# Loads, decay rounds and TensorE's order moved in a kernel of RWKV-7 attention and hash routing

## The chip, the cores and the metric

The kernel runs on one core of a Trainium2 chip. The metric is the device time of one execution in microseconds, the median of three runs. A core has five engines that run side by side, each with its own queue of instructions in order: TensorE (PE in the profile; its weight loads are PEld), VectorE (DVE), ScalarE (ACT), GpSimd (POOL) and SyncE (SP). Transfers are issued from the queues of SyncE, GpSimd and ScalarE and run on sixteen DMA engines.

## The reference, cut to what matters

Two blocks follow each other. The first is a recurrence over 768 tokens for 4 x 8 heads with 40 x 40 states:

```python
def _attn_ref(r, k, v, w, a, b):
    state = np.zeros((B, H, D, D), dtype=np.float32)        # B, H, S, D = 4, 8, 768, 40
    for t in range(S):
        kt, vt, rt = (k[:, :, t], v[:, :, t], r[:, :, t])
        wt, at, bt = (w[:, :, t], a[:, :, t], b[:, :, t])
        y[:, :, t] = np.einsum('bhd,bhde->bhe', rt, state)
        Sa = np.einsum('bhde,bhe->bhd', state, at)
        state_decay = state * wt[:, :, None, :] - np.einsum('bhd,bhe->bhde', Sa, bt)
        state = state_decay + np.einsum('bhd,bhe->bhde', vt, kt)
    return y
```

The second sends each of the 3072 rows to one of 8 experts by a hash of its token and applies two layers, `np.maximum(xe @ w1[e], 0.0) @ w2[e]`, with w1 320 x 1024 and w2 1024 x 320. The change touches the first block alone.

## The kernel before

The recurrence is computed in chunks of 64 tokens. A *tile* is one chunk of two batches (128 partitions); there are 24 of them. A tile passes two halves. The first half forms `at` and `z` (a, b and k multiplied by products of decays), turns both on TensorE, forms the scores `a` between tokens, and with three other tiles (a *group*) inverts the triangular part of the scores on VectorE. The second half follows 8 *ticks* later: it applies the inverse, updates the state and makes the output y. So for 24 ticks TensorE does the second half of one tile beside the first half of the tile that is 8 later.

All steps are entered in a plan with a tick, and the plan is then sorted, so that a number decides where a step stands in each engine's queue. `STEPS` gives the places within a tick:

```python
STEPS = ["r1", "z", "y", "nc", "x", "at_t", "x_t", "s", "u", "sd", "a", "r_t", "r0", "rc"]

def at_tick(tick, step=None, order=0):
    if step is not None:
        tick += STEPS.index(step) / len(STEPS)
    ...
# [cut]
with tc.manual_schedule(engines={ET.PE, ET.DVE, ET.Activation, ET.Pool}):
    for *_, f in sorted(plan, key=lambda e: e[:3]):
        f()
```

The products of decays, p and q, are made for two chunks at a time, in 6 *rounds*. A round loads w, multiplies up a tree (`todo`), gets the other half's product by a small matmul (`f_ps`), and goes down the tree again for p and for q (`then`). Round 0 keeps p and q in SBUF for tiles 0 to 3 and stores p for later; the other rounds store both to DRAM, from where the tiles load them:

```python
def decays(ri, t_w, t0, span, t_f, span_f=None, stores=None):
    ...                                         # [cut] load w; todo: the products, up to x["own"]
    @then.append
    def _():
        x["f_ps"] = p = bank([P, D], "f_ps")
        nc.tensor.matmul(p, lhsT=partner[:], rhs=x["own"][:], start=True, stop=True)
    ...                                         # [cut] ends, reciprocal, spread of pb
    @then.append
    def _():
        spread(x["pb"], True, (0,))
        if ri == 0:
            x["p"] = p_rows = turned_rows(x["pb"][:], early.tile([P, 2 * BLK * BLK], F32, tag="nu", name="p_rows"))
            at_tick_later.append(lambda: nc.sync.dma_start(pq_dram[ri][0].rearrange("t bh e -> t (bh e)"), p_rows))
        elif stores is None:
            store(0, x["pb"][:])
    ...                                         # [cut] the same for q; en_ps and pend
    if ri == 0:
        then = then[:3] + then[5:7] + then[3:5] + then[7:]
        at_tick_later = []
        at_tick(1.36)(lambda: [f() for f in at_tick_later])
    if stores is not None:
        at_tick(stores)(lambda: (store(0, x["pb"][:]), store(1, x["qb"][:])))
    for i, f in enumerate(todo):
        at_tick(t0 + span * i / len(todo), order=8)(f)
    for i, f in enumerate(then):
        at_tick(t_f[i] if isinstance(t_f, tuple) else t_f + span_f * i / len(then), order=8)(f)
```

The inputs of a tile are six transfers on SyncE's queue, 64 x 8 pieces of 40 numbers each. Two tiles borrow buffers that later steps use:

```python
    @at_tick({0: -3.9, 1: -3.8, 2: -2.8, 3: -2.7}.get(u, max(u - 2.55, t_mult_of(u - 2) + 0.03)))
    def _():
        kb_tag = {2: "x_t", 3: "mr"}.get(u)
        ...                                     # [cut] kb from tag kb_tag or "kb" (2 buffers)
        x["a"] = al = work.tile([P, DM], F32, tag="py" if kb_tag else "al", name="al")
        load(lambda be, rows: by_head(al, rows), a, 2 * g, n * C)
        load(lambda be, rows: by_head(kb[:, be], rows), b, 2 * g, n * C)
        load(lambda be, rows: by_head(kb[:, be], rows), k, 2 * g, n * C, crossed=True)
```

The inversion of a group takes the single buffer `nu`, which is also the buffer of `row` and of round 0's `p_rows`:

```python
def group_i(gi, t0, t1, t2):
    @at_tick(t0 - 0.5, order=9)
    def _():
        x["nu"] = nu = early.tile([P, 2, BLK * BLK], F32, tag="nu", name="nu")
        ...                                     # [cut]
        nc.gpsimd.memset(ub, 0.0)
    @at_tick(t0, order=9)
    def _():
        nc.vector.transpose(paired(x["n"])..., paired(x["pk"])...)
    ...                                         # [cut] 30 pairs: outer = u * n; u += outer; then ut
# [cut]
for gi in range(NU // GRP):
    t0 = gi * GRP + GRP - 1 + t_a               # t_a = STEPS.index("a") / len(STEPS)
    group_i(gi, t0 + 0.05, t0 + 0.1, t0 + 3.4)
```

In a tick with both halves TensorE's chain is: rc (scores of r with x), which VectorE masks to `mr`; y, which needs `mr` and `sd`; nc, which needs the copy `r1`; x and u (the inverse); x_t (x turned, after ScalarE has copied it out of nc); s (the state, which VectorE multiplies to `st`); sd (`st` turned); a (which needs `z_t` and `at_t`), of which ScalarE copies `pk` and `no` and VectorE masks `mk`. Of the PSUM buffers, z, nc, x_t, sd, a and rc share two of two banks each, in turn.

## Time and profile before

| | us |
|---|---|
| median of 3 runs | 647.45 |
| lowest, highest | 645.55, 648.0 |
| span of the profiled run | 645.1 |

| engine | busy us | share |
|---|---|---|
| TensorE, matmul | 556.3 | 86% |
| TensorE, weight loads | 422.7 | 66% |
| VectorE | 351.6 | 55% |
| ScalarE | 293.7 | 46% |
| GpSimd | 195.8 | 30% |

The page divides the span into 40 slices of 16 us and gives the busy share of each in tenths; TensorE has 4 to 6 in slices 2 to 5 and 8 or 9 from slice 7 on. In the first slices the granted clock of TensorE falls to 0.5. "Releaser" in the views below is what ended an engine's wait; "issue" is time in which the engine waited for nothing that the profile shows. A row of a timeline has the start, the length, the engine, the line, what it does, and in brackets the idle time before it.

### The profile page before, as it was taken

How to read it: one execution, taken by the hardware profiler on the slowest of the kernel's cores; microseconds unless marked ns; L12 is line 12 of the kernel's file. 1: busy time of each engine (PE TensorE's matmuls, PEld its weight loads, DVE VectorE, ACT ScalarE, POOL GpSimd, SP SyncE). 2: the span in 40 equal slices, each digit the busy share in tenths (PEclk: the TensorE clock that was granted, in tenths of full speed). 3: DMA queues.
4: the chain of work that ended last, by engine and by line, in shares of the span. 5: the costliest groups of instructions: out<-in, count | busy, mean ns of one | idle time of the engine just before them, and what ended most of it. 6: DMA issues, size and time to landing. Idle time of an engine off the chain costs nothing.

```text
span 645.1 us, 22962 instructions
## 1 busy us (share of the span) xinstructions
PE 556.3 (86%) x9866; PEld 422.7 (66%) x9866; DVE 351.6 (55%) x920; ACT 293.7 (46%) x695; POOL 195.8 (30%) x331
## 2 busy tenths in 40 slices
PE   0443568988999999999899998999999999999995
PEld 0332457877787878888788887666565646565552
DVE  6968679966977896797798553232021202203010
ACT  4162436757776677777767661113131304101100
POOL 0631341535333344432423321261313131230101
PEclk9975559989999999999999999999999999999999
DMA  8999988987797687842434613697333373220000
GB/s 160 198 197 178 163 154 143 190 144 137 149 184 148 129 169 149 153 97 45 103 60 116 155 53 97 223 290 248 110 102 113 105 264 103 66 96 20 30 12 25
DMA packets 195770, 85.13 MB, mean 132 GB/s; under 512 B 176718, under 2 KB 186191, under 8 KB 195664
## 3 DMA queue, kind: packets, MB, share of 16 engines
q1 hardware_dynamic: 184016, 45.59, 37.6%
q0 software_dynamic: 11456, 37.37, 20.1%
q8 instruction: 78, 1.28, 0.9%
q10 hardware_dynamic: 192, 0.66, 0.4%
q14 instruction: 28, 0.23, 0.1%
HBM read 66.54 MB, written 15.40 MB: 127 GB/s over the span
## 4 chain that ended last, share of the span: by engine, by line
PE 50%; issue 23%; DVE 10%; DMA 6%; SPq 5%; POOL 4%; ACT 2%; POOLq 0%; DVEq 0%; ACTq 0%
PE up_ps L1057 6%; PE dn_ps L1075 6%; PE y_ps L291 5%; PE s_ps L291 4%; PE rc_ps L291 3%; PE r_ps L291 3%; SPq L310 3%; PE x_t_ps L733 3%; PE a_ps L291 3%; PE t_ps L573 3%; PE sd_ps L793 3%; PE z_ps L521 2%; POOL out_dram L1080 2%; DVE mr L745 2%; PE nc_ps L291 2%
## 5 line engine op out<-in xcount | busy, mean ns | idle before, releaser
L1065 DVE TENSOR_SCALAR ht<-up_ps 128x416 f32<-128x416 f32 (+2 forms) x36 | 19.4, 543 | 165.2 <-PE up_ps L1062 163.7
L1075 PE MATMUL dn_ps<-w,ht 128*128 128x320 f32 x336 | 91.7, 433 | 0.0
L1057 PE MATMUL up_ps<-xt,w 128*128 128x416 f32 x224 | 81.3, 516 | 0.0
L1075 PEld LDWEIGHTS dn_ps<-w,ht 128*128 128x128 f32 x336 | 63.3, 190 | 25.5
L1080 POOL DMA_INDIRECT out_dram<-o,idx_all x26 | 26.1, 1004 | 165.4 <-ACT o L1079 164.3
L785 POOL DMA_DIRECT2D x_rows<-xs x44 | 23.2, 535 | 171.3 <-DVE xs L781 96.5
L1067 ACT ACTIVATE ht<-up_ps 128x416 f32<-128x416 f32 (+2 forms) x36 | 17.2, 478 | 107.5 <-PE up_ps L1062 107.4
L1057 PEld LDWEIGHTS up_ps<-xt,w 128*128 128x128 f32 x224 | 41.9, 190 | 36.8 <-issue 31.7
L615 DVE TENSOR_TENSOR outer<-nu 128x252 f32<-128x252 f32 (+8 forms) x180 | 63.4, 352 | 4.9
L622 DVE TENSOR_TENSOR nu<-nu,outer 128x252 f32<-128x252 f32 (+8 forms) x180 | 63.4, 352 | 4.3
L1079 ACT COPY o<-dn_ps 128x320 f32<-128x320 f32 x26 | 11.1, 425 | 92.4 <-PE dn_ps L1075 92.4
L521 PE MATMUL z_ps<-ident,z 128*104 128x128 f32 x192 | 31.2, 315 | 24.2 <-DVE z L507 21.4
L525 ACT COPY z_t<-z_ps 104x512 f32<-104x512 f32 x48 | 25.7, 588 | 47.4 <-PE z_ps L521 46.3
L521 PEld LDWEIGHTS z_ps<-ident,z 128*104 128x104 f32 x192 | 24.5, 150 | 27.1 <-issue 23.2
L468 POOL DMA_DIRECT2D ql<-q_rows x48 | 25.1, 531 | 48.4 <-DVE pb L377 15.4
L723 ACT COPY x<-nc_ps 64x320 f32<-64x320 f32 x48 | 20.1, 420 | 42.7 <-PE nc_ps L291 42.1
L745 DVE TENSOR_TENSOR mr<-rc_ps,after 128x1024 f32<-128x1024 f32 x24 | 29.3, 1220 | 13.6 <-PE rc_ps L291 13.6
L291 PE MATMUL rc_ps<-r_t,x_t 64*64 64x64 f32 x1536 | 30.1, 222 | 6.7 <-issue 6.0
L291 PE MATMUL a_ps<-at_t,z_t 64*64 64x64 f32 x1536 | 32.3, 241 | 3.6 <-ACT at_t L574 2.4
L291 PEld LDWEIGHTS a_ps<-at_t,z_t 64*64 64x64 f32 x1536 | 28.6, 152 | 8.1 <-ACT at_t L574 3.6
L548 DVE TENSOR_TENSOR mk<-a_ps,after 128x512 f32<-128x512 f32 x24 | 16.6, 690 | 28.9 <-ACT no L565 26.2
L291 PEld LDWEIGHTS rc_ps<-r_t,x_t 64*64 64x64 f32 x1536 | 25.7, 134 | 9.3 <-issue 6.1
(230 smaller groups left out, 1125.9 us busy)
## 6 DMA issues: line engine op xcount, KB each, us to landing
ql<-q_rows POOLq DMA_DIRECT2D x48, 160.0 KB, 4.3
w<-in_moe_w_dram SPq DMA_DIRECT2D x10, 640.0 KB, 7.6
w<-in_moe_w_dram SPq DMA_DIRECT2D x10, 512.0 KB, 4.3
al<-in_a_dram SPq DMA_DIRECT2D x48, 80.0 KB, 4.2
pl<-p_rows POOLq DMA_DIRECT2D x48, 80.0 KB, 4.5
r<-in_r_dram SPq DMA_DIRECT2D x48, 80.0 KB, 3.8
x<-in_v_dram SPq DMA_DIRECT2D x48, 80.0 KB, 3.7
py<-p_rows POOLq DMA_DIRECT2D x48, 80.0 KB, 4.8
```

The lines of the kernel that those rows point to most:

```text
L291: nc.tensor.matmul(out_, lhsT=lhsT, rhs=rhs, start=start, stop=stop, skip_group_check=True)
L468: nc.gpsimd.dma_start(ql[half(be)], of_batches(rows_of_chunk("q"), 2 * g, 2))
L521: nc.tensor.transpose(p[0:R, be, hp * P:(hp + 1) * P], x["z"][:, be, hp, :], ident[:])
L525: nc.scalar.copy(t[0:R, be].rearrange("p h t -> p (h t)"), p[0:R, be])
L615: nc.vector.tensor_tensor(tv, paired(x["u"])[:, 0:full[1], j:j + 1, :].to_broadcast(full), paired(x["n"])[:, j // 2, j + 1:, j % 2].unsque ...
L622: nc.vector.tensor_tensor(o, o, x["t"][:, 0:n].rearrange("p (c i k) -> p c i k", c=full[1], k=2), op=OP.add)
L723: nc.scalar.copy(x["x"][half(be), be].rearrange("p (a q) (two e) -> p a (q two) e", a=2, two=2)[:, :, :, 0:D], p[half(be), :, 0:HP * D].re ...
L745: nc.vector.tensor_tensor(t[:].rearrange("p two h t -> p (two h) t"), p[:].rearrange("p two (h t) -> p (two h) t", t=C), after[:].unsqueez ...
L785: dma(x_of[2 * g + be, n * C:(n + 1) * C], xs[half(be), :])
L1057: nc.tensor.matmul(p[:], lhsT=w1[c][:, (f0 + i) * P:(f0 + i + 1) * P], rhs=xt[:, c, 0:n], start=(c == 0), stop=False)
L1075: nc.tensor.matmul(p[i * m:(i + 1) * m], lhsT=ht[:, f, c0:c0 + m], rhs=w2[f // (FP // 2)][:, f % (FP // 2), :], start=(f == 0), stop=(f == ...
L1080: st = nc.gpsimd.indirect_dma_start(out=out[:], out_offset=bass.IndirectOffsetOnAxis(ap=idx, axis=0), in_=o[0:m], in_offset=None, bounds_c ...
```

## The change

It moves steps in the plan; the arithmetic is the same. The inputs of tiles 4 to 7 are to be loaded at the time of the first tiles, with the borrowed buffers used a second time by tiles 6 and 7; the store of round 0's p goes behind them. Rounds 3 to 5 of the decays are to stand between two inversions instead of within one. On TensorE, z of the next tile goes between r0 and rc, at_t to the place behind r1, and sd between x and x_t.

```diff
-    STEPS = ["r1", "z", "y", "nc", "x", "at_t", "x_t", "s", "u", "sd", "a", "r_t", "r0", "rc"]
+    STEPS = ["r1", "at_t", "y", "nc", "x", "sd", "x_t", "s", "u", "a", "r_t", "r0", "z", "rc"]
...
-            at_tick(1.36)(lambda: [f() for f in at_tick_later])
+            at_tick(3.2)(lambda: [f() for f in at_tick_later])
...
-            at_tick(t_f[i] if isinstance(t_f, tuple) else t_f + span_f * i / len(then), order=8)(f)
+            at_tick(t_f + span_f * i / len(then) if span_f else t_f[i], order=8)(f)
...
     def t_mult_of(u):
-        return u + LATE[u] - 0.1 if u in LATE else u - 0.6
+        return u + LATE[u] - 0.2 if u in LATE else u - 0.6
...
-        @at_tick({0: -3.9, 1: -3.8, 2: -2.8, 3: -2.7}.get(u, max(u - 2.55, t_mult_of(u - 2) + 0.03)))
+        @at_tick({0: -3.9, 1: -3.8, 2: -2.8, 3: -2.7, 4: 0.9, 5: 1.5, 6: 2.0, 7: 2.5}.get(u, max(u - 2.55, t_mult_of(u - 2) + 0.03)))
         def _():
-            kb_tag = {2: "x_t", 3: "mr"}.get(u)
+            kb_tag = {2: "x_t", 3: "mr", 6: "x_t", 7: "mr"}.get(u)
...
-        @at_tick(u - 0.4 if ahead else u + late, None if ahead else "z")
+        @at_tick(u - 0.4 if ahead else u - 1 + late, None if ahead else "z")
...
     for ri in range(3, NR):
-        t0 = ri * RN * NG - 5.0
-        decays(ri, t0 - 2.0, t0 + 0.25, 1.0, t0 + 1.3, 1.1)
+        t0 = ri * RN * NG - 4.9
+        decays(ri, t0 - 2.1, t0, 0.12, [t0 + f for f in (0.13, 0.2, 0.21, 0.25, 0.35, 0.42, 0.5, 0.55)])
```

## The prediction

> **What bounds the kernel now.** I read the page's first two parts, then the busy time by stretches, then the timelines of single engines, and the table of waits last. The stretches, each row with its length and then the busy microseconds of TensorE, its weight loads, VectorE, ScalarE and GpSimd:

> ```profile
> core 0: us, PE busy (x) PEld busy (x) DVE busy (x) ACT busy (x) POOL busy (x), PEclk, DMA share, GB/s
> 0.00:47.00 47.00, 15.03 (x313) 12.95 (x313) 34.75 (x98) 20.13 (x62) 15.11 (x34) 0.94 0.98 184
> 47.00:88.00 41.00, 16.44 (x246) 14.30 (x248) 32.04 (x80) 14.11 (x34) 9.60 (x20) 0.50 0.97 162
> ...
> 262.00:310.00 48.00, 46.41 (x1366) 40.13 (x1368) 37.72 (x94) 35.89 (x85) 17.32 (x34) 1.00 0.46 88
> ...
> 395.00:645.00 250.00, 239.80 (x1018) 148.43 (x1018) 46.93 (x146) 46.44 (x94) 61.97 (x70) 0.99 0.38 122
> ```

> There are three regimes. Up to about 88 us VectorE leads (78% busy from 47 to 88 us, TensorE 40%). From 110 to 395 us TensorE is nearly full. The last 250 us are the expert layers, whose instructions the change leaves in the same order on TensorE. So the time is about: when TensorE becomes dense, plus its work and its stalls in the ticks, plus 250.

> The start, on the queue of SyncE, on GpSimd and on VectorE (start, length, engine, line, what; in brackets the idle time before and its releaser):

> ```profile
> 34.71 4.63 SPq L339 DMA_DIRECT2D q_rows<-qb  x4
> 39.39 1.71 SPq L408 DMA_DIRECT2D p_rows<-p_rows  x1
> 41.15 1.67 SPq L310 DMA_DIRECT2D al<-in_a_dram  x2
> ```
> ```profile
> 44.63 0.95 POOL L591 MEMSET nu<- 128x1024 f32 x1 [1.22 <-DMA p_rows<-p_rows]
> ```
> ```profile
> 46.98 1.25 DVE L597 STREAM_TRANSPOSE nu<-pk 128x1024 f32<-128x1024 f32 x1 [1.21 <-ACT pk L564]
> ...
> 78.85 0.49 DVE L500 SCALAR_TENSOR_TENSOR at<-al,pl 128x320 f32<-128x320 f32 x1 [3.26 <-DMA al<-in_a_dram]
> 81.31 0.83 DVE L507 TENSOR_TENSOR z<-kb,ql 128x640 f32<-128x640 f32 x1 [1.97 <-DMA kb<-in_k_dram]
> ...
> 87.62 1.20 DVE L631 STREAM_TRANSPOSE ut<-nu 128x1024 f32<-128x1024 f32 x1
> ```

> The first inversion runs on VectorE from 46.98 to 88.82 us. In it VectorE waits 3.26 + 1.97 = 5.2 us for the inputs of tile 7. And the buffer `nu` of the inversion is the buffer that held p of round 0: GpSimd's clearing of it waited for the store of p (line 408) to land, at 44.6 us, 5.2 us after its issue began. That wait was harmless.

> TensorE's waits from 88 to 310 us (in total, times, longest):

> ```profile
> PE r_ps L291 <- issue: 5.7, 4, 2.0
> PE rc_ps L291 <- issue: 5.3, 6, 2.3
> PE x_ps L291 <- DVE ut L630: 3.5, 1, 3.5
> PE y_ps L291 <- DVE mr L745: 1.9, 3, 1.0
> ```

> Only 1.9 us are for mr. The large entries, "issue", break off in the middle of a group (rc stops after 53 of its 64 at 133.8 us), so they aren't data.

> [...]78 instruction packets carry 1.28 MB, and the stalls stand where a, r0, rc and r1 use up instructions fastest. [...]0.50 from 47 to 88 us, and after the 2.26 us stall at 133.8 us eight z transposes took 1.88 us instead of 1.01. [...]

> **The change part by part.** No instruction is added or removed; everything is order.

> 1. Inputs of tiles 4 to 7 at ticks 0.9 to 2.5. Removes VectorE's waits for tile 7: -5.2 us. The z of tiles 4 to 6 stand slightly earlier against the inversion, which I put at -0.4 us of the 1.66 us that mk waits there (1.08 and 0.58), but the mk of tile 6, which used to be hidden behind the wait for tile 7, then waits about 0.5 us. Net -5.1.

> 2. The store of p moves from tick 1.36 to 3.2. In the built program it stands on SyncE's queue behind the loads of tiles 4 to 7 and the stores of round 1, and the inversion's first transpose (line 597) waits for its completion. Step by step: tile 4's loads wait for the at of tile 0, done at 26.4 us; six DMAs at about 0.7 us each, to 31. The stores of round 1's p take 4.2 us as now, to 35.2; its q 4.6 to 5, to 40. Then the loads of tiles 5, 6 and 7, which take 4.0 to 5.9 us a tile in this trace (tiles 0 to 3: 4.0 to 4.8), so 3 x 4.6 = 14, to 54. Then the store, 5.2 us to its landing: 59 (57 to 62). VectorE is ready for line 597 at about 47.6, so it sits idle for some 11 us, and the inversion starts 12 us late. With part 1 it ends at 88.8 + 12 - 5.1 = 95.7 us: +6.9.

> 3. Rounds 3 to 5 of the decays between inversions. VectorE's work in a round, by the rows of round 1 (22.18 to 34.60 us): products 2.5, ends 0.9, p 2.2, q 2.2, so about 7.8 us. It now stands in a block behind ut, where VectorE used to idle (3.61 us before mk at 95.2, 3.30 at 149.5), which is the aim. But the small matmul f_ps, which needs the products, now stands on TensorE right after nc and before x. In a steady tick, counted from the end of rc: TensorE reaches f_ps after r1 0.70, at 0.58, y 1.61 and nc 0.60, at 3.5 us. VectorE has mr to 1.2, two last small steps, ut 2 x 1.2 to 4.2 (at 136.5 to 140.6 it took just that), products 2.5 and xs 0.45: 7.1 us. So TensorE stalls 3.6 us[...]. Then mk and the next transposes come late: VectorE's block ends 14.7 us after rc, so rc, which now takes over the PSUM buffer of a, waits some 0.3 us, and mr 0.3 more. I put 5 us on each of rounds 4 and 5, less 0.9 of "issue" stall[...]: +8. In round 3, at the start, x of tile 0 begins 3.0 us after ut instead of 1.07 before its end; the at transpose of tile 7 (1.1) now lies ahead, and z of tile 8 as before. Along xi, um (1.7), u, a, r_t, r0, z, r1, at and nc at half clock I get nc 14.9 us after ut, against 9.3 plus the 0.6 of at: +5.

> 4. Order on TensorE. A tick's own work doesn't change: r1 0.70, at 0.58, y 1.61, nc 0.60, x 0.62, sd 0.82, x_t 0.87, s 1.28, u 0.62, a 1.09, r_t 0.59, r0 0.70, z 1.01, rc 1.09 = 12.2 us. The 16 ticks from 106.8 to 314.6 us took 13.0 each; some 0.8 is stall. With z between r0 and rc, two stretches of many short matmuls are parted by 1 us with few instructions, and r_t has longer to be copied. I expect a third to a half of the "issue" stalls to go: -5. sd between x and x_t covers the 0.86 us copies of x, which matters in the last eight ticks: -1.5.

> Sum: 6.9 + 5 + 8 - 5 - 1.5 = +13.4, so 647.5 + 13.4 = 661.

> **The rivals.** First, the store lands early enough, because SyncE's queue runs faster than I reckon. For it: SyncE idles from 21 to 30 us. Against: 18 loads lie between the q stores and the store of p, and none in this trace went faster than 0.63 us in a row, so even then it isn't issued before 51 us and lands at 56: 3 us less, 658. Second, the stalls at f_ps don't come, because VectorE runs ahead: before, it waits 24.5 us in all for a's copies ahead of mk. Against: that wait ties it to TensorE in the very tick before ut. Without the stalls: 653. Third, the order on TensorE frees all of the 5.7 + 5.3 + 1.9 = 12.9 us of stalls before r, rc and y; with the second rival that would be 653 - (12.9 - 5) = 645. Fourth, a late first tick that also delays the fetch and holds the clock at half for longer: 670.

> **Range and chances.** The delay of the first inversion is seen in the program's waits and is nearly certain; its size is 10 to 15. The stalls at f_ps are reckoned, 0 to 12. The gain on TensorE is the least sure, 0 to 12. Together 648 to 672. The line of +2% is 660.4, just below my number: slower by over 2% 0.52, within 2% 0.42, faster by over 2% 0.06.

> **What would show it.** Right: line 597 starts near 59 us with a wait on the DMA of p_rows; no VectorE wait for al or kb up to 96 us; f_ps waits for own about 3.5 us three times; mk has hardly any waits in those ticks; the first y at about 120 us rather than 108. Wrong: line 597 near 47 us, or TensorE without waits on own, or ticks without "issue". If the first y comes before 108 us, the whole of the first half is wrong, and the time falls below 640.

## The result, and the profile after

| | before | after |
|---|---|---|
| median, us | 647.73 | 665.62 |
| lowest, highest, us | 645.55, 648.74 | 663.64, 667.06 |
| ratio (95% interval) | | 1.0279 (1.0241 to 1.0317) |

The change costs 18 us, 2.8%. The busy time by stretches of the kernel after, with the same columns as in the prediction (stretch, length, busy microseconds of TensorE, its weight loads, VectorE, ScalarE and GpSimd, granted clock, DMA):

```profile
0.00:61.00 61.00, 16.25 (x312) 14.26 (x312) 34.80 (x97) 21.16 (x64) 13.16 (x30) 0.84 0.95 173
61.00:98.00 37.00, 17.22 (x241) 15.04 (x241) 32.56 (x80) 13.65 (x32) 11.57 (x23) 0.50 0.85 148
272.00:320.00 48.00, 46.91 (x1440) 40.59 (x1436) 40.09 (x97) 36.98 (x87) 17.75 (x35) 1.00 0.54 106
415.00:665.00 250.00, 239.80 (x1018) 148.35 (x1018) 47.03 (x146) 46.48 (x94) 62.03 (x70) 1.00 0.38 122
```

The expert layers took their 250 us as before. In the first 61 us each engine does about what it did in the first 47 us before; those 14 us are idle. SyncE's queue shows why (start, length, engine, line, what):

```profile
29.86 1.36 SPq L310 DMA_DIRECT2D kb<-in_k_dram  x2
31.32 6.97 SPq L339 DMA_DIRECT2D p_rows<-pb  x4
38.39 4.79 SPq L339 DMA_DIRECT2D q_rows<-qb  x4
43.23 1.75 SPq L310 DMA_DIRECT2D al<-in_a_dram  x2
...
55.60 1.31 SPq L310 DMA_DIRECT2D kb_mr<-in_k_dram  x2
56.96 0.62 SPq L408 DMA_DIRECT2D p_rows<-p_rows  x1
```

The store of round 0's p is issued at 56.96 us, behind three tiles of loads. GpSimd's clearing of `nu`, and then VectorE's first transpose of the inversion, wait for it to land:

```profile
61.13 0.95 POOL L591 MEMSET nu<- 128x1024 f32 x1 [13.83 <-DMA p_rows<-p_rows]
```
```profile
61.12 1.25 DVE L597 STREAM_TRANSPOSE nu<-pk 128x1024 f32<-128x1024 f32 x1 [12.73 <-DMA p_rows<-p_rows]
...
97.10 1.20 DVE L631 STREAM_TRANSPOSE ut<-nu 128x1024 f32<-128x1024 f32 x1
```

Before, line 597 stood at 46.98 us with a wait of 1.21; the inversion ends at 98.3 us instead of 88.8. No wait of VectorE for `al` or `kb` is left in it. TensorE's waits from 98 to 320 us (in total, times, longest):

```profile
PE f_ps L384 <- DVE own L365: 11.7, 3, 5.3
PE rc_ps L291 <- issue: 3.6, 3, 2.0
...
PE r_ps L291 <- issue: 0.9, 2, 0.6
...
PE y_ps L291 <- DVE mr L745: 0.6, 2, 0.3
```

The three stalls at `f_ps` are there, and the entries "issue" have shrunk. What an "issue" stall waits for can be read from the same traces. In the kernels before and after, the instruction packets of the queue q8 are of 16 KiB (78 of them, 1.28 MB in all); 40 come between 120 and 310 us, one every 4.8 us. In these two kernels all 24 such stalls of TensorE between 100 and 400 us end 1.2 to 1.7 us after the transfer of such a packet has ended; in the fourteen traces of this case 145 of 164 do, while of the matmuls without a stall only about one in nine starts at such a moment. By this timing they are waits for instructions, as the prediction took them to be.

The loss is best laid out between three marks: the first `mr` of VectorE (the start), the sixteenth (the middle, ticks with both halves; 24 tiles that are 8 apart give 16 of these, not 24), and the first matmul of the experts (the tail, in which the first half of the tiles has run out). Before, the start took 108.9 us, the middle 205.8, the tail 81.2. What the kernels of the main comparison took more or less than that, in microseconds of one profiled execution, with "issue" stalls and half-clock time in the middle:

| kernel | start | middle | tail | issue, middle | half clock, middle |
|---|---|---|---|---|---|
| before | 0 | 0 | 0 | 13.4 | 3.4 |
| after | +13.1 | +2.9 | +4.1 | 5.8 | 6.8 |
| TensorE's order alone | +0.4 | +4.8 | +5.6 | 6.0 | 17.1 |
| decays alone | +2.8 | +2.5 | +4.4 | 5.8 | 13.7 |
| loads and store alone | +8.6 | -2.1 | +4.8 | 10.3 | 0 |
| loads alone | -4.0 | -3.6 | +3.5 | 8.5 | 0 |
| after, store back | -0.8 | +4.6 | +6.6 | 6.2 | 10.2 |

Two kernels that share their code up to a mark still differ there: three kernels with the start of "after" reached the first `mr` at 119.2, 119.7 and 122.0 us, and from there to the fifteenth, again with the same code, they took 193.3, 191.6 and 194.3 us. So a difference under 3 us in one cell says nothing by itself.

### The profile page after: what moved, and what is told of

It is laid out like the page before. It is cut to its first block, busy times and chain, and to the rows that moved or that the text cites. A ratio compares the mean times of both kernels' runs of the same rounds, so it can differ in the third digit from the quotient of the medians.

```text
span 665.3 us, 22958 instructions
## 1 busy us (share of the span) xinstructions
PE 563.3 (85%) x9866; PEld 428.6 (64%) x9866; DVE 356.0 (54%) x920; ACT 295.6 (44%) x695; POOL 196.1 (29%) x331
## 3 DMA queue, kind: packets, MB, share of 16 engines
q8 instruction: 78, 1.28, 0.8%
## 4 chain that ended last, share of the span: by engine, by line
PE 47%; issue 21%; DVE 11%; SPq 7%; POOL 4%; ACT 4%; DMA 4%; POOLq 0%; DVEq 0%; ACTq 0%
PE up_ps L1058 6%; PE dn_ps L1076 6%; PE y_ps L291 5%; SPq L310 4%; PE s_ps L291 4%; PE x_t_ps L733 3%; PE rc_ps L291 3%; PE a_ps L291 3%; PE sd_ps L793 3%; PE x_ps L291 2%; DVE mr L745 2%; POOL out_dram L1081 2%; PE nc_ps L291 2%; SPq L339 2%; PE r_ps L291 2%
## 5 line engine op out<-in xcount | busy, mean ns | idle before, releaser
L1066 DVE TENSOR_SCALAR ht<-up_ps 128x416 f32<-128x416 f32 (+2 forms) x36 | 19.4, 543 | 165.0 <-PE up_ps L1063 163.4
L1081 POOL DMA_INDIRECT out_dram<-o,idx_all x26 | 26.1, 1005 | 165.0 <-ACT o L1080 163.9
L745 DVE TENSOR_TENSOR mr<-rc_ps,after 128x1024 f32<-128x1024 f32 x24 | 29.3, 1220 | 13.5 <-PE rc_ps L291 13.5
L384 PE MATMUL f_ps<-own,partner 128*128 128x40 f32 x12 | 3.4, 381 | 38.3 <-DVE own L365 38.3
L291 PE MATMUL a_ps<-at_t,z_t 64*64 64x64 f32 x1536 | 33.0, 242 | 2.7 <-ACT at_t L574 2.7
L291 PE MATMUL rc_ps<-r_t,x_t 64*64 64x64 f32 x1536 | 29.3, 221 | 7.0 <-issue 4.7
L291 PEld LDWEIGHTS rc_ps<-r_t,x_t 64*64 64x64 f32 x1536 | 25.3, 134 | 11.6 <-DVE mk L548 4.8
L291 PEld LDWEIGHTS a_ps<-at_t,z_t 64*64 64x64 f32 x1536 | 29.1, 154 | 5.7 <-ACT at_t L574 3.9
```

The lines of the kernel that those rows point to most:

```text
L291: nc.tensor.matmul(out_, lhsT=lhsT, rhs=rhs, start=start, stop=stop, skip_group_check=True)
L745: nc.vector.tensor_tensor(t[:].rearrange("p two h t -> p (two h) t"), p[:].rearrange("p two (h t) -> p (two h) t", t=C), after[:].unsqueez ...
L1081: st = nc.gpsimd.indirect_dma_start(out=out[:], out_offset=bass.IndirectOffsetOnAxis(ap=idx, axis=0), in_=o[0:m], in_offset=None, bounds_c ...
```

## The experiments

All ratios are to the kernel before, run on the same chip in the same set, with their 95% intervals. The ratio on record is not the quotient of the medians given here; for runs 6 to 8, beside a kernel before of 644.97 us, the quotient is 0.4 to 0.5% lower.

**1. TensorE's order alone** on the kernel before.

```diff
-    STEPS = ["r1", "z", "y", "nc", "x", "at_t", "x_t", "s", "u", "sd", "a", "r_t", "r0", "rc"]
+    STEPS = ["r1", "at_t", "y", "nc", "x", "sd", "x_t", "s", "u", "a", "r_t", "r0", "z", "rc"]
-        return u + LATE[u] - 0.1 if u in LATE else u - 0.6
+        return u + LATE[u] - 0.2 if u in LATE else u - 0.6
-        @at_tick(u - 0.4 if ahead else u + late, None if ahead else "z")
+        @at_tick(u - 0.4 if ahead else u - 1 + late, None if ahead else "z")
```

> The kernel before with TensorE's order alone (the list of steps, z one tick earlier, and the 0.2 that z's product needs for it). My theory: the stalls called issue fall from 13 to about 5 us as in the changed kernel, and the last eight ticks lose about 4 us because y reaches mr earlier; the start is as before. So 644 us (641 to 647). Rival: the order gains nothing by itself and the fewer issue stalls of the changed kernel come from TensorE standing still elsewhere; then 648 to 652.

Measured: 656.19 us, 1.0117 (1.0020 to 1.0214). Both theories missed: the order doesn't gain anything, it costs some 8 to 9 us. Its trace says where. TensorE reaches the second part of y at about 167 us, with `mr` not there yet. VectorE from `mk` to `mr` in that tick:

```profile
163.06 0.69 DVE L548 TENSOR_TENSOR mk<-a_ps,after 128x512 f32<-128x512 f32 x1 [1.56 <-ACT no L565]
163.66 0.38 DVE L615 TENSOR_TENSOR outer<-nu 128x220 f32<-128x220 f32 x1
163.96 1.36 DVE L377 TENSOR_TENSOR pb<-pb 128x40 f32<-128x40 f32 x4
165.23 0.38 DVE L622 TENSOR_TENSOR nu<-nu,outer 128x220 f32<-128x220 f32 x1
...
166.44 0.82 DVE L377 TENSOR_TENSOR pb<-pb,wt 128x640 f32<-128x640 f32 x1
167.18 0.40 DVE L615 TENSOR_TENSOR outer<-nu 128x240 f32<-128x240 f32 x1
167.50 1.22 DVE L745 TENSOR_TENSOR mr<-rc_ps,after 128x1024 f32<-128x1024 f32 x1
```
```profile
168.77 1.13 PE L291 MATMUL y_ps<-z,mr 128*64 128x40 f32 x32 [1.81 <-DVE mr L745]
```

The scores rc are done at 165.0 us; 2.2 us of the decays' p (line 377) and the steps of the inversion stand in front of `mr`. Before, z's transposes (1.0 us) stood between rc and y and a stall "issue" (1.46 us at 166.8) fell there too, which hid the same delay. The wait of 1.8 us comes three times (110, 169 and 227 us), and behind each the clock halves, once for 3.4 us and twice for 6.8: 17.1 us at half clock in the middle, against 3.4. In the kernel after, the decays are no longer between `mk` and `mr`, and these waits are gone. So these two parts of the change cost less together than apart: beside a kernel before of 647.47 us the order alone took 656.19 us, the decays alone 656.48 (run 2), and both with the early loads no more than 656.30 (run 4).

**2. The rounds of decays alone** on the kernel before (the last two hunks of the change: `t0 = ri * RN * NG - 4.9` and the list of times).

> The kernel before with the decay rounds 3 to 5 between the inversions alone. My theory: in three ticks TensorE waits for the products of decays at f_ps (3 to 5 us each, 11 us in all), of which some is won back because the ticks after are free of decays; 655 us (651 to 660), and waits of f_ps on own in the trace. Rival: the rounds fill what VectorE idled before and cost nothing; then 646 to 649 and the loss is all from the store.

Measured: 656.48 us, 1.0124 (1.0042 to 1.0205), within the theory's range and far from the rival's. The two long ticks took 19.2 and 20.0 us (before 15.7 and 14.2). TensorE's waits from 100 to 320 us:

```profile
PE rc_ps L291 <- issue: 5.3, 8, 1.9
PE f_ps L384 <- DVE own L365: 5.0, 2, 3.7
PE y_ps L291 <- DVE mr L745: 1.5, 3, 0.8
PE r_ps L291 <- issue: 0.6, 1, 0.6
```

With a first stall at `f_ps` of 6.79 us, which ends at 91.9 us, ahead of this window, the three come to 11.8 us, as expected; at that place x used to wait 3.5 us for `ut`. The order on TensorE is the old one here, and "issue" falls to the same sum as in the kernel after (5.8 us in the middle of each). This matters below.

**3. Loads and store alone** on the kernel before (both early loads and `at_tick(3.2)`).

> The kernel before with the early loads and the late store of p alone. My theory: the first transpose of the inversion starts at 59 to 62 us instead of 47, behind the landing of p, and the inversion then loses its 5 us of waits for tile 7, so the start is 8 to 10 us later and nothing else changes: 656 us (654 to 659). Rival: the late inversion is hidden, because TensorE is not yet dense there; then 645 to 650.

Measured: 656.92 us, 1.0139 (1.0049 to 1.0228). The first transpose waits as it does in the kernel after:

```profile
60.60 1.25 DVE L597 STREAM_TRANSPOSE nu<-pk 128x1024 f32<-128x1024 f32 x1 [14.57 <-DMA p_rows<-p_rows]
```

**4. The kernel after with the store back in its old place.**

```diff
-            at_tick(3.2)(lambda: [f() for f in at_tick_later])
+            at_tick(1.36)(lambda: [f() for f in at_tick_later])
```

> The changed kernel with the store of p at tick 1.36 again, ahead of the loads of tiles 5 to 7. My theory: it lands at about 48 us, the inversion starts at 48 to 49 instead of 61, and the time falls by what VectorE waited, 11 to 12 us: 654 us (652 to 656). Rival: the loads of tiles 6 and 7 now come later and VectorE waits for them instead, so less than half of it is won: 660 us or more.

Measured: 656.30 us, 1.0114 (1.0030 to 1.0198), 0.3 us beside the theory's range and far from the rival's. The transpose stands at 47.19 us, with no wait shown:

```profile
47.19 1.24 DVE L597 STREAM_TRANSPOSE nu<-pk 128x1024 f32<-128x1024 f32 x1
```

One number accounts for 9 to 11 of the 18 us (9.3 by the medians, 1.65% by the ratios). By the table it takes 13.9 us off the start; middle and tail give some 4 us of it back.

**5. The early loads alone** (the store stays at 1.36).

> The kernel before with one part of the change: the inputs of tiles 4 to 7 early; the store of p stays at tick 1.36. My theory (the loads take VectorE's two waits for tile 7, 5.2 us, out of the first inversion, and that start sets the end): 642.5 us, 640.5 to 645, with the first inversion's first transpose at about 47 us and its end near 84 us. Rival (the end of the inversion isn't what the ticks wait for; the early loads crowd out other transfers and a later wait takes back what is won): 646 to 650.

Measured: 642.78 us against 644.97 in this set, 0.9968 (0.9943 to 0.9994). The inversion ends 4.0 us earlier, and both waits for tile 7 are gone, but only 2 us arrive at the end. With run 3, the store alone is +1.7% of the time; the same follows from the kernel after and run 4 (2.8 less 1.1). Alone and in company it costs the same, as far as these intervals, of about 0.9 each, can tell.

**6. sd alone moved** to between x and x_t.

> The kernel before with sd alone moved from between u and a to between x and x_t; z and at_t stay. My theory (the new order has two losses: moving sd costs the tail, moving z away from between rc and y uncovers the wait for mr in the first ticks of the inversions): sd alone costs the tail only, 651 us, 649.5 to 653, with no y wait for mr over 1.2 us from 88 to 310 us. Rival (sd's move alone also tightens VectorE's way from st to mr in the middle ticks): 654 to 658 with y waits of 1.5 us or more there. A third: nothing, 646 to 649.

Measured: 649.96 us, 1.0119 (1.0074 to 1.0163). The time is within the theory's range, but not for its reason: the profiled execution lost nothing in the tail (+0.2 us), though y waited 1.93 us for `mr` there, and y waited 1.4 us at 109 us, which the theory excluded.

**7. z and at_t alone moved** (sd stays).

> The kernel before with z moved between r0 and rc and at_t behind r1 (and the loads' late ticks 0.1 earlier, as the change has it); sd stays. My theory: y waits for mr some 1.8 us at the first ticks of three inversions and the clock halves behind each; the tail is as before; against this some 6 us less of issue stalls on TensorE: 652 us, 650 to 654.5. Rival (the whole loss of the new order is sd's, and z between r0 and rc only wins issue stalls): 641 to 646.

Measured: 650.92 us, 1.0142 (1.0095 to 1.0190). The time and half of the theory hold: "issue" in the middle falls from 13.4 to 2.8 us, and y waits for `mr` 1.79, 1.31 and 1.80 us at 110, 169 and 224 us. The middle is as long as before, to 0.1 us. But the tail lost 3.9 us with sd where it was, so the tail's loss isn't sd's alone.

**8. The kernel after with sd back between u and a, from tile 14 on.**

```diff
-            @at_tick(t0 + 1, "sd")
+            @at_tick(t0 + 1 + (3.5 / len(STEPS) if u >= NU - 10 else 0), "sd")
```

> The kernel after, with sd of tiles 14 to 23 alone back between u and a (ticks 23 and later, where no z is left to stand between s and rc). My theory (in those ticks TensorE reaches y before VectorE has got from st through the routing's small steps, mk and the first transpose to mr; the wait of 2.6 us halves the clock for a window): the wait for mr at the tick of 332 us falls to about 1 us, x_t and the steps behind it run at full clock, and the kernel takes 661.6 us, 660 to 663.5. Rival (that tick is slow by the routing's steps or by a late a and not by the place of sd): 664 to 667.

Measured: 661.52 us, but in a set whose kernel before took 644.97: 1.0293 (1.0254 to 1.0331; the medians give 1.0257), not shown to be better than the 1.0279 of the kernel after. The number is the one expected and the theory fell all the same: y still waits 1.78 us (instead of 2.62), the clock still halves (0.50 from 328.31 to 335.14 us), and the tick takes 12.6 us (13.4).

**9. The kernel after with the routing's steps of tick 23 in ticks 24 to 26.** These are small steps on VectorE that prepare the second block's choice of experts.

```diff
-        t = ([4.5, 15.63, 15.95, 19.63, 19.631, 19.632, 23.63, 23.631, 23.632] + ...
+        t = ([4.5, 15.63, 15.95, 19.63, 19.631, 19.632, 24.6, 25.6, 26.6] + ...
```

> The kernel after, with the three blocks of small routing steps of tick 23 (VectorE, 4 us) moved to ticks 24, 25 and 26; TensorE's order is the same. Theory (these steps stand between st and mk in the one tick that has no z behind r0, so mr is late, and the wait of 2.6 us is enough to halve the clock): the wait for mr falls below 0.5 us, the tick of 13.4 us falls to about 10, and the kernel takes 661.5 us, 660 to 663.5. Rival (the tick is slow through something else, or the steps only delay a later tick): 664 to 667.

Measured: 666.90 us, 1.0323 (1.0260 to 1.0386). The rival was right: the steps delay later ticks, one after the other. TensorE's rows at the waits for `mr`:

```profile
326.04 1.13 PE L291 MATMUL y_ps<-z,mr 128*64 128x40 f32 x32 [1.96 <-DVE mr L745]
...
339.12 1.13 PE L291 MATMUL y_ps<-z,mr 128*64 128x40 f32 x32 [1.85 <-DVE mr L745]
...
350.61 1.13 PE L291 MATMUL y_ps<-z,mr 128*64 128x40 f32 x32 [1.88 <-DVE mr L745]
```

And at tick 24 itself 1.96 us remain with no routing step in the way: `mk`, the transpose of line 597 and the first four steps of the inversion are enough.

**10. The kernel after with f_ps of rounds 3 to 5 between x_t and s.**

```diff
-... (0.13, 0.2, 0.21, 0.25, 0.35, 0.42, 0.5, 0.55)
+... (0.36, 0.37, 0.38, 0.385, 0.39, 0.42, 0.5, 0.55)
```

> The kernel after, with the small matmul f_ps of rounds 3 to 5 moved from in front of x to between x_t and s. The prediction's reading (TensorE's 3.2 us at f_ps and the half clock behind it are the cost of a decay tick): the stalls go, the two long ticks fall from 18.6 to about 13.5 us, the start gains 3 more: 652 us, 650 to 655. Rival (VectorE is what is full in these ticks: the decays' 7.8 us stand in one block between ut and mk, so mk comes only some 1.7 us earlier and TensorE waits for it at rc instead): the two ticks stay at 16 to 18 us, with a wait of over 1 us at rc for mk, and the kernel takes 659 to 664.

Measured: 657.43 us, 1.0164 (1.0121 to 1.0207): between the two. The start is 5.5 us shorter than in the trace of the kernel after, and 2.7 to 5.5 shorter than in the three traces with that start; 3 were expected. The two ticks fell from 18.6 and 18.7 to 16.4 and 16.8, in the rival's range, and VectorE shows why. From the end of the inversion to the next one's first transpose it doesn't stand still once (no row of this stretch has an idle time):

```profile
146.10 1.20 DVE L631 STREAM_TRANSPOSE ut<-nu 128x1024 f32<-128x1024 f32 x1
147.23 0.45 DVE L368 TENSOR_TENSOR pb<-wt 128x320 f32<-128x320 f32 x1
...
153.44 0.83 DVE L377 TENSOR_TENSOR pb<-pb,wt 128x640 f32<-128x640 f32 x1
154.18 0.55 DVE L762 TENSOR_TENSOR st<-s_ps,pend 104x160 f32<-104x160 f32 x2
154.64 1.36 DVE L379 TENSOR_TENSOR qb<-qb 128x40 f32<-128x40 f32 x4
156.03 0.82 DVE L379 TENSOR_TENSOR qb<-qb,wt 128x640 f32<-128x640 f32 x1
156.78 0.68 DVE L548 TENSOR_TENSOR mk<-a_ps,after 128x512 f32<-128x512 f32 x1
157.38 1.24 DVE L597 STREAM_TRANSPOSE nu<-pk 128x1024 f32<-128x1024 f32 x1
```
```profile
157.51 1.16 PE L291 MATMUL rc_ps<-r_t,x_t 64*64 64x64 f32 x64 [1.66 <-DVE mk L548]
```

TensorE's wait has moved from `f_ps` to rc (in the second long tick it is 1.28 us, put down there to `z_t`): VectorE is full in these ticks, and that sets them. In the kernel after it does stand still between `ut` and line 597, for 0.51, 0.97 and 0.66 us in the first long tick. These 2.1 us are what run 10 took off that tick (2.2 us).

**11 and 12. Towards a version that beats both.** Run 11 is run 5 with the routing's steps moved as in run 9; run 12 adds z and at_t of run 7 and puts the decays' p behind `mr`.

```diff
-        decays(ri, t0 - 2.0, t0 + 0.25, 1.0, t0 + 1.3, 1.1)
+        decays(ri, t0 - 2.0, t0 + 0.25, 1.0, tuple(t0 + f for f in (1.3, 1.44, 1.57, 1.96, 1.97, 2.11, 2.25, 2.3)))
```

> The kernel before with the early loads alone and the routing's steps of tick 23 later: a version to beat both. If the half clock in tick 24 is what took 3.5 us of the early loads' gain back: 640 us, 637.5 to 642. If not: 642.5 to 645.

> The version of the run above, with z also between r0 and rc and at_t behind r1 (sd stays), and the decays' product p of rounds 3 to 5 moved from between mk and mr to behind mr. Theory (z there saves some 8 to 10 us of issue stalls, and what it lost was the wait of y for mr in the decay ticks, 5.5 us and two half-clock windows): 635 us, 632 to 638.5. Rival (issue stalls and waits for mr trade places whatever stands where): 640 to 646.

Measured: 647.23 us, 0.9977 (0.9948 to 1.0005), and 651.21 us, 1.0070 (1.0043 to 1.0098). Neither time lies in a range that had been given. Run 11 gained nothing over run 5. Both lose in the tail, 4.7 and 5.6 us against the kernel before: y waits for `mr` 1.13 and 1.49 us at 325 and 336 us in run 11, and 1.61, 1.57 and 1.68 us at 312, 325 and 336 us in run 12; those at 325 and 336 us fall in the ticks to which the routing's steps were moved, as in run 9. The middle of run 12 took only 0.5 us more than before. There the waits of 1.8 us for `mr` halved, as meant, and others took their place, because the p products now stand ahead of `at` and `z`:

```profile
227.62 1.05 PE L521 MATMUL z_ps<-ident,z 128*104 128x128 f32 x8 [0.58 <-DVE z L507]
229.84 1.16 PE L291 MATMUL rc_ps<-r_t,x_t 64*64 64x64 f32 x64 [1.16 <-ACT z_t L525]
...
233.92 1.13 PE L291 MATMUL y_ps<-z,mr 128*64 128x40 f32 x32 [0.92 <-DVE mr L745]
```

The rival ("trade places whatever stands where") covers the direction, not the size. The early loads alone remain the only version ahead of the kernel before, by 0.3% with an interval that ends just below 1.

## Why the prediction was right, step by step, and where it was not

The time (661 predicted, 665.6 measured) and the cause of its largest part were right. The sum, with what the profiled executions show for each term:

| term of the sum | predicted | measured |
|---|---|---|
| inversion ends later | +6.9 | +9.5 |
| f_ps ahead of x at the start | +5 | +3.6 |
| ticks of rounds 4 and 5 | +8 | +7.4 |
| the other ticks of the middle ("order on TensorE") | -5 | -4.5 |
| sd and the last ticks | -1.5 | +4.1 |
| sum | +13.4 | +20.1 |

The measured terms: 98.3 less 88.8 us for the inversion; the first `mr` 13.1 us later, of which 9.5 are already counted; 18.6 - 15.7 and 18.7 - 14.2 us; the rest of the middle's +2.9; the tail. The sum is that of two profiled executions; the medians are 17.9 apart. Most of what the number fell short by came in the tail, and the tail's loss can't be put down to the change (below), so how close the number came is in part luck. For the second row the traces give a range: from the end of the inversion to the first `mr` the four kernels with the new order and `f_ps` ahead of x took 22.8 to 23.7 us, against 20.1 before, so 2.7 to 3.6.

Two sums of the prediction are off, without an effect on its total. From 106.8 to 314.6 us there are 15 ticks and not 16, so a tick took 13.9 us, and 1.7 of them, not 0.8, were more than TensorE's own 12.2. And the second rival's 653 takes off the 8 us of rounds 4 and 5 but not the 5 at the start; with them it is 648.

*Store and loads.* Right, and shown by runs 3 to 5. The mis-sized term is the store of round 1's p, "4.2 us as now": its issue took 6.97 us here, so line 597 stood at 61.1 us and not at 59. That isn't chance: in the nine traces in which the loads of tile 4 are issued just ahead of it it took 6.0 to 7.3 us, in the five others 3.6 to 5.1. The loads gave back 4.0 us (run 5), not 5.1.

*f_ps.* The three stalls came, of 5.3, 3.2 and 3.2 us where 3.6 had been reckoned for a tick, with 3.4 us of half clock behind each of the two in the ticks. But they aren't the cause of the long ticks as the prediction told it. Run 10 took nearly all of the stalls in the ticks away and the ticks kept over half of their excess over a quiet tick of 13 us; the larger part, 3.4 of the first tick's 5.6 us, is VectorE's work from `ut` to `mk`, which the prediction had reckoned ("14.7 us after rc") and then given only 0.6 us of waits. At the start, the stall at `f_ps` itself counts.

*TensorE's order.* This step failed, although its number looks right. The prediction put -5 us down to z between r0 and rc. Run 7 shows that "issue" falls with it (13.4 to 2.8 us), but the middle didn't get shorter by it, and alone the order costs 1.2% (run 1). And run 2, with the old order, has the same low "issue" and the same middle (+2.5 us against +2.9). So the -4.5 us of the other ticks came with the move of the decays just as well: up to the fifteenth `mr` these ticks are 6.9 us shorter than before in run 2, and 5.0, 6.1 and 8.9 us in the kernel after and in runs 8 and 9, whose code is the same there. And runs 4 and 2, which differ by the order and the early loads alone, took 656.30 and 656.48 us beside the same kernel before; as the early loads are worth some 2 us (run 5), the order cost about 2 us beside the decays (an estimate), where -5 had been predicted. Why "issue" falls where TensorE stands still elsewhere, no run shows.

*The tail.* No gain of 1.5 us is to be seen, and the tick behind the sixteenth `mr` lost 3.6. That tick before, and in the kernel after:

```profile
315.95 1.13 PE L291 MATMUL y_ps<-z,mr 128*64 128x40 f32 x32 [1.05 <-DVE mr L745]
...
318.28 1.10 PE L733 MATMUL x_t_ps<-ident,x 128*128 128x128 f32 x8
```
```profile
331.94 1.94 PE L291 MATMUL y_ps<-z,mr 128*64 128x40 f32 x32 [2.62 <-DVE mr L745]
...
337.19 1.74 PE L733 MATMUL x_t_ps<-ident,x 128*128 128x128 f32 x8
```

The copies of x that sd was to cover were not what bound there; `mr` was. TensorE has 0.8 us less to do between s and y, VectorE has just as much, y waits 2.62 us instead of 1.05, and the clock halves (0.50 from 331.79 to 338.61 us): y takes 1.94 us instead of 1.13, x_t 1.74 instead of 1.10. Sd isn't alone in this. In the same tick y waits 1.93 us with sd alone moved (run 6), 1.94 with z and at_t alone (run 7) and 2.36 with both (run 1); with sd put back it waits 1.78 (run 8), with the routing's steps out of the way 1.96 (run 9). But the larger loss is the half clock, and that can't be put down to the change. Run 5, whose tail has the old code, lost 2.9 of its 3.5 us in the same tick (last section). Runs 2 and 3, whose tail is old too, lost 4.4 and 4.8 us, most of it at an "issue" stall of 2.1 and 2.7 us near 375 us and the half clock behind it. So of the four traces with the old code in the tail only that of the kernel before kept its clock there, and the table measures against a lucky one. How often each kernel meets it over many executions stays open. Each execution's mean clock tells only the total: run 5 stood at half clock for 56 us in the mean of its executions and the kernel before beside it for 59 (both estimates), so run 5 doesn't meet more of it as a rule.

*The rivals.* The first fell (the store didn't land earlier but later), the second fell, as the `f_ps` stalls came, and the third fell by run 1. The fourth (a late start that holds the clock at half for longer) has its part: half clock lasted from 41.7 to 110 us instead of to 96.

## What to carry to other kernels

Before a buffer's last reader is moved, find out who takes the buffer next: here a store whose wait had been harmless was put behind 18 loads, and the next owner was the first inversion, 42 us of VectorE's time on which the ticks wait. Where two engines are both nearly full, a stall that is taken away can turn up at the next wait (run 10: 3.2 us at `f_ps` in each long tick, then 1.66 and 1.28 at rc): add up the other engine's work in the same stretch first. And a part of a change tested alone can cost more than in company (the order: some 9 us alone, about 2 beside the decays), so an effect belongs to a pair until a run has separated it.

## What the runs showed of the hardware

```profile
133.65:137.06 3.41, 1.15 (x36) 0.92 (x28) 1.69 (x6) 0.82 (x3) 0.00 (x0) 1.00 0.69 107
```

Nor were most windows idle in the long half clock from 41.5 to 96 us, with TensorE busy for up to 2.7 us of a window; there the clock rose behind the first window that was busy throughout (92.7 to 96.1 us). In run 6 it took two such windows (110.99 to 117.82 us).

Windows of three kernels around the tick behind the sixteenth `mr`, first the loads alone (run 5), where an issue stall of 0.69 us and a wait of 1.06 us fall in one window. These windows are cut 0.14 us behind the grid; on the grid itself, where the clock changes at 308.29 us, TensorE is busy for 1.70 us of the first:

```profile
305.02:308.43 3.41, 1.65 (x42) 1.26 (x36) 3.17 (x7) 1.10 (x3) 0.00 (x0) 0.98 0.48 104
308.43:311.85 3.42, 3.42 (x88) 3.27 (x90) 2.29 (x9) 0.42 (x1) 0.75 (x2) 0.50 0.24 97
311.85:315.26 3.41, 3.41 (x32) 2.44 (x28) 0.99 (x3) 3.12 (x7) 1.34 (x3) 0.52 0.40 101
```

Then the kernel before, where the same two stalls fall in two windows, and the clock stays up:

```profile
311.15:314.56 3.41, 2.72 (x108) 2.35 (x104) 2.96 (x10) 2.30 (x7) 0.00 (x0) 1.00 0.32 50
314.56:317.97 3.41, 2.35 (x96) 2.10 (x94) 3.16 (x9) 0.41 (x2) 0.05 (x1) 1.00 0.51 161
```

And sd alone (run 6), where a wait of 1.93 us lies across a boundary:

```profile
312.36:315.77 3.41, 1.72 (x48) 1.49 (x48) 3.17 (x6) 0.77 (x2) 0.00 (x0) 1.00 0.41 58
315.77:319.19 3.42, 3.10 (x105) 2.97 (x106) 3.06 (x11) 1.20 (x3) 1.14 (x3) 1.00 0.37 140
```

The first number after the length is TensorE's busy time, the third from the end the clock. With 1.70 us of 3.41 busy the next two windows ran at half; with 1.72 they did not. In the fourteen traces here, between 105 and 410 us, all 22 windows that began at full clock and had TensorE busy for less than half (1.70 us) were followed by half clock; of those between 1.7 and 2.5 us ten were and most weren't. A window at half clock costs up to 1.7 us, half of its 3.41 us (an estimate). The two stalls above, 1.75 us together, cost run 5 another 2.9 us (a tick of 12.7 us instead of 9.8), while the kernel before, with the same two stalls in two windows, kept its clock.
